# Chunks 0 and 1 of a chunked DeltaNet: block forward substitution with three sweeps in place of joins and cross products

## The chip, the cores and the metric

One NeuronCore of a Trainium2 chip. The metric is the device time of one execution in microseconds; the median of 3 runs of the kernel before is 568.46 us (568.26 to 570.27).

## The reference, cut to what matters

```
def _attn_ref(q, k, v, beta):              # B, H, S, D = 4, 8, 768, 48
    k_n = k / (norm(k) + 1e-06)
    for t in range(S):
        y[t] = q[t] @ state
        state = state + beta[t] * outer(k_n[t], v[t] - k_n[t] @ state)
def _moe_ref(x, w_in, w_out):              # 3072 x 384, 384 x 2048, 2048 x 384
    h = x @ w_in
    return (max(h, 0) + log1p(exp(-abs(h)))) @ w_out
```

The rows y of all heads, side by side, are x of the second part. Everything is fp32.

## The kernel before, in words

The sequence is cut into 12 chunks of 64 tokens (C). The 32 head sequences lie as 16 slots (NP) of two. Within a chunk the recursion is a triangular system of 64 unknowns per head: with L the strictly lower part of the scaled gram matrix K K^T, the corrected values are U = (I + L)^-1 (v - K state); y and the next state follow by products. The systems of two chunks are solved together (`invert(u)`, u = 0 for chunks 0 and 1): a transpose puts head and block into partitions, `norms` makes the scales, and a loop of two element-wise operations per row (L335, L339) inverts the diagonal blocks. For u = 0 the blocks are 16 wide (N16 = 1, QB = 16) and the loop runs on VectorE, from u = 1 on 32 wide and on GpSimd (ON_POOL).

For u = 0, `turn_back` and `turn` transpose the inverses back, `join(s)` (two sets of small products, L363 and L372, and a subtraction) makes 32-wide inverses out of 16-wide ones, and `cross_a`, `arrange`, `cross_b` make the 64-wide inverse TT. The operands of the joins are spread from the grams by `copy_below`, `below_half` and `spread`. `first_p`, `first_mask`, `first_u`, `first_y` are the first chunk's products, with no state yet. `u_all` gives U of later chunks.

The expert layer runs in passes; pass 0 is chunk 0 alone, in 8 steps t = 0 to 7 of two weight tiles f each. At each step the order written into every engine's queue is: `hidden` (products, L682), `convert` (weights put together, VectorE L639), the blocks that `at(t, ...)` has planned for t, `softplus`, `top` (high halves of the next weights, ScalarE L629), `low` by the table LOWS (low words of a weight for split products, L659), `output` of the step before (L728), the blocks of t + 0.5, `high` by HIGHS. Pass 1 (chunk 1, from t = 8) needs low words; pass 0 does not. Chunk 1's own work is planned into steps 0 to 6, the solve of chunks 2 and 3 (u = 1) starts at step 0 and its end is due at step 8 (END, DONE). Every engine takes its queue in order.

The weights come by `feed(n)`, n half tiles of 384 KB on the queue of SP, which also carries k, q, v and beta. PSUM has 8 banks: ph0, ph1 for `hid`, po0 to po2 for outputs (po2 lent to `bank` by turns in pass 0), three "pa". `warm` runs products of constants whose results nobody reads.

Of the kernel before, what the change touches and what calls it, by code (L numbers as in the profile page):

```python
# [36 lines left out]
LOWS = {6: (0,), 7: (1, 2, 3), 8: (4, 5, 6), 9: (7,), 10: (8, 9, 10), 11: (11,), 12: (12, 13), 13: (14, 15)}  # L37
# [22 lines left out]
def deltanet_moe(ctx, tc, kT, qT, kI, vN, beta, wts, out, outT):  # L60
# [53 lines left out]
    half = const.tile([P, 1], F32, name="half")  # L114
    sides = const.tile([P, 2], F32, name="sides")
    W, HF, RA, RB, OFF, TT, LTD, LDS, NN, NV, X, PK, bet, kts = ({} for _ in range(14))
# [4 lines left out]
    NT, LB = {}, {}  # L121
# [33 lines left out]
    def below(u):  # L155

        LB[u] = one.tile([P, 3, NP, C], F32, name=f"x{u + 1}")
        nc.vector.memset(LB[u][:, 0:2, :, 0:QB], 0.0)
        nc.vector.memset(LB[u][:, 0:2, :, HB:HB + QB], 0.0)
        nc.gpsimd.memset(LB[u][:, 2, :, QB:HB], 0.0)  # L160
        nc.gpsimd.memset(LB[u][:, 2, :, HB + QB:], 0.0)

    def spread(u, s):
        for h in range(2):
            nc.scalar.activation(LB[u][:, s, :, HB * h + QB:HB * h + HB],
                                 LTD[u][:, s * NP:(s + 1) * NP, QB:], AF.Copy,
                                 scale=sides[:, h:h + 1])
# [117 lines left out]
    def transpose_norms(u):  # L285
        nn, nt = NT[u]
        nc.vector.transpose(nn, nt)
        nc.vector.tensor_scalar(nn, nn, 0.5, None, op0=ALU.mult)
        for j in range(2):
            NN[2 * u + j] = nn[:, j * NP:(j + 1) * NP]  # L290

    def diagonal(t, blocks, n, r0, c0, nr, nc_, wide=(True, True)):

        dims = [t.ap[0]] + ([(n * (HB + 1), len(blocks))] if len(blocks) > 1 else [])
        dims += [(HB if wide[0] else 0, nr), (1 if wide[1] else 0, nc_)]
        return bass.AP(t.tensor, t.offset + r0 * HB + c0, dims)

    def invert(u):
# [22 lines left out]
        else:  # L321
# [6 lines left out]
        (nc.scalar.copy if u < N16 else engine.tensor_copy)(  # L328
            Z.rearrange("p a b -> p (a b)")[:, 0:HB * HB:HB + 1], cT)
# [14 lines left out]
    def turn_back(u, n=HB):  # L344
        nc.vector.transpose(TT[u][:, :, HB:HB + n].rearrange("p q c -> p c q"),
                            Z[:, :, 0:n].rearrange("p c j -> p j c"))
# [9 lines left out]
    def join(s):  # L356

        u, j = divmod(s, 2)
        tt = TT[u][:, j * NP:(j + 1) * NP, :]
        pw = bank([P, NP, QB])  # L360
        for p in range(NP):
            for r in tk:
                nc.tensor.matmul(pw[r, p, :], LB[u][r, j, p, :], tt[r, p, HB:HB + QB],  # L363
                                 start=True, stop=True)
        for h in range(2):
            nc.scalar.activation(LB[u][:, 2, :, HB * h:HB * h + QB], pw, AF.Copy,
                                 scale=sides[:, h:h + 1])
        yield
        pz = bank([P, NP, QB])
        for p in range(NP):  # L370
            for r in tk:
                nc.tensor.matmul(pz[r, p, :], LB[u][r, 2, p, :], tt[r, p, QB:HB],  # L372
                                 start=True, stop=True)
        yield
        nc.vector.tensor_tensor(tt[:, :, QB:HB], tt[:, :, QB:HB], pz, op=ALU.subtract)
        nc.vector.transpose(tt[:, :, HB:], tt[:, :, 0:HB])
        yield

    def cross(s, product, emptied):


        n = 2 if s < 1 else 1
        pms = [bank([P, NP // 2, HB]) for _ in range(n)]
        for i, e, p, ab, t in quads:
            a, b = product(p, t)
            nc.tensor.matmul(pms[t % n][(lo, hi)[e][t], i, :], a, b, start=True, stop=True)
        for e in range(2):
            for t in range(2):
                emptied(e, t, pms[t % n][(lo, hi)[e][t]])

    def cross_a(s):
# [3 lines left out]
        def emptied(e, t, pm):  # L395
            o = parity(OFF[s])[lo[t], e]
            if s < 1 and t:
                nc.vector.tensor_scalar(o, pm, -1.0, None, op0=ALU.mult)
            else:
                nc.scalar.activation(o, pm, AF.Copy, scale=-1.0)  # L400
# [40 lines left out]
    def cross_b(s):  # L441
# [3 lines left out]
              lambda e, t, pm: copies[s < 1 and t](parity(tt)[lo[t], e, :, HB:], pm))  # L445
# [48 lines left out]
    def first_u():  # L494

        pu = [bank([P, B, D])] + [bank([P, 2, NK, D]) for g in range(2)]

        def product(to, b, hh):
            p, e = 4 * b + hh, hh % 2
            for ab in range(2):  # L500
                t, h = ab ^ e, ab ^ (hh == NK)
                nc.tensor.matmul(to[tk[h]], TT[0][tk[t], p, :], NV[0][tk[t], p, :],
                                 start=True, stop=True)

        for g in range(2):
            for b in range(2):
                for k, hh in enumerate((0, 2, NK)):
                    product(pu[1 + g][:, b, k, :], 2 * g + b, hh)
                    if g == 0 and k < 2:
                        product(pu[0][:, 2 * b + k, :], 2 * b + k, 1)  # L510
        for g in range(2):
            bs = slice(2 * g, 2 * g + 2)
            for ab in range(2):
                copies[ab](still[tk[ab], ab, bs, 0:NK:2, 0:D], pu[1 + g][tk[ab], :, 0:2])
                copies[ab](still[tk[1 - ab], ab, bs, :, D:],
                           pu[1 + g][tk[1 - ab], :, 2].rearrange("p b (t c) -> p b t c", t=NK))
                if g == 0:
                    copies[ab](still[tk[ab], ab, :, 1, 0:D], pu[0][tk[ab]])
# [7 lines left out]
    def first_y():  # L526

        X[0] = one.tile([P, NK, 1, 1, B, C], F32, name="x0")
        for g in range(2):
# [6 lines left out]
            copies[g](X[0][:, :, 0, 0, 2 * g:2 * g + 2, :],  # L536
                      py.rearrange("p (b t) c -> p t b c", t=NK))
        load_q(1)
# [247 lines left out]
    still = one.tile([P, 2, B, NK, C], F32, name="ot")  # L786

    def warm(*columns):

        pw = bank([P, 512])  # L790
        for m in columns:
            nc.tensor.matmul(pw[:, 0:m], even[:, 0:P], even[:, 0:m], start=True, stop=True)  # L792

    with tc.manual_schedule(engines={ET.PE, ET.DVE, ET.Activation, ET.Pool, ET.SP}):
# [14 lines left out]
        feed(14)  # L809
# [5 lines left out]
        nc.vector.memset(still, 0.0)  # L815
        warm(512, 256)
        nc.gpsimd.memset(Z, 0.0)
        nc.gpsimd.memset(big[:, 2 * NP * QW:], 0.0)
        nc.gpsimd.memset(half, 1.0)
        nc.gpsimd.memset(sides, 0.0)  # L820
        for h in range(2):
            nc.gpsimd.memset(sides[lo[h], 0:1], 1.0)
            nc.gpsimd.memset(sides[hi[h], 1:2], 1.0)
        systems(0)
        below(0)
# [280 lines left out]
```

## Time and profile before, and how to read it

| | |
|---|---|
| median of 3 runs | 568.46 us |
| the profiled execution | 568.94 us |
| its span | 567.2 us |
| TensorE / VectorE / ScalarE / GpSimd busy | 547.4 / 367.0 / 362.9 / 201.9 us |
| mean granted TensorE clock | 0.987 |

PE is TensorE, PEld its weight loads, DVE VectorE, ACT ScalarE, POOL GpSimd, SP the queue that issues transfers. "L682" is line 682 of the kernel. An fp32 product shows as two records. A row of the timeline gives start and length in us from the span's start, the engine, line, operation, output and inputs, the number of instructions that it merges, and in brackets the idle time before it and what ended it.

### The profile page before, as it was taken

How to read it: one execution, taken by the hardware profiler on the slowest of the kernel's cores; microseconds unless marked ns; L12 is line 12 of the kernel's file. 1: busy time of each engine (PE TensorE's matmuls, PEld its weight loads, DVE VectorE, ACT ScalarE, POOL GpSimd, SP SyncE). 2: the span in 40 equal slices, each digit the busy share in tenths (PEclk: the TensorE clock that was granted, in tenths of full speed). 3: DMA queues.
4: the chain of work that ended last, by engine and by line, in shares of the span. 5: the costliest groups of instructions: out<-in, count | busy, mean ns of one | idle time of the engine just before them, and what ended most of it. 6: DMA issues, size and time to landing. Idle time of an engine off the chain costs nothing.

```text
span 567.2 us, 17501 instructions
## 1 busy us (share of the span) xinstructions
PE 547.4 (96%) x7447; PEld 450.1 (79%) x7447; DVE 367.0 (65%) x657; ACT 362.9 (64%) x713; POOL 201.9 (36%) x354
## 2 busy tenths in 40 slices
PE   6889899799999999999999999999999999999997
PEld 4668677589997888887888888788888888888885
DVE  8847784799947777448947467947375647343434
ACT  4627788698857973755873756863647855455353
POOL 7111688207982058811688001797000000000000
PEclk9969999899999999999999999999999999999999
DMA  9977511213340122220122220021320030010001
GB/s 206 346 288 251 143 30 44 59 58 71 88 101 2 31 60 69 60 85 14 31 59 71 55 90 15 2 67 32 72 85 3 2 71 1 15 57 1 2 0 55
DMA packets 35501, 39.55 MB, mean 70 GB/s; under 512 B 22528, under 2 KB 25216, under 8 KB 35424
## 3 DMA queue, kind: packets, MB, share of 16 engines
q1 hardware_dynamic: 35280, 38.18, 23.6%
q8 instruction: 58, 0.95, 0.7%
q10 hardware_dynamic: 144, 0.26, 0.1%
q14 instruction: 19, 0.16, 0.1%
HBM read 31.55 MB, written 4.72 MB: 64 GB/s over the span
## 4 chain that ended last, share of the span: by engine, by line
PE 79%; POOL 7%; DVE 6%; ACT 3%; DMA 3%; issue 2%; ACTq 0%; DVEq 0%; POOLq 0%
PE po L728 32%; PE ph L682 31%; POOL Z L339 3%; PE pa L587 3%; POOL tmp L335 3%; PE pa L454 2%; PE pa L413 2%; DMA kt<-kT 2%; PE pa L556 2%; PE pa L792 1%; DMA big<-qT 1%; PE pa L568 1%; DVE a L659 1%; PE ph L568 1%; PE ph L249 1%
## 5 line engine op out<-in xcount | busy, mean ns | idle before, releaser
L682 PE MATMUL ph<-x,b 128*128 128x512 f32 (+1 forms) x576 | 166.5, 373 | 0.0
L687 ACT ACTIVATE a<-ph 128x512 f32<-128x512 f32 x96 | 57.4, 598 | 159.4 <-PE ph L682 156.9
L682 PE MATMUL ph<-x,a 128*128 128x512 f32 (+1 forms) x384 | 129.5, 375 | 4.4 <-DVE a L659 3.7
L694 DVE SCALAR_TENSOR_TENSOR a<-ph,a 128x512 f32<-128x512 f32 x88 | 60.5, 687 | 93.6 <-ACT a L689 93.2
L682 PEld LDWEIGHTS ph<-x,b 128*128 128x128 f32 x576 | 105.2, 188 | 19.2
L728 PE MATMUL po<-gh,b 128*128 128x512 f32 (+1 forms) x241 | 97.6, 405 | 1.4 <-DVE gh L696 1.4
L339 POOL TENSOR_TENSOR Z<-Z,tmp 128x30 f32<-128x30 f32 (+9 forms) x150 | 90.1, 601 | 11.8
L728 PE MATMUL po<-gh,a 128*128 128x512 f32 (+1 forms) x241 | 94.0, 390 | 0.0
L335 POOL TENSOR_TENSOR tmp<-Z,ltq 128x30 f32<-128x30 f32 (+9 forms) x150 | 85.2, 568 | 11.4
L682 PEld LDWEIGHTS ph<-x,a 128*128 128x128 f32 x384 | 72.3, 189 | 17.6 <-DVE a L659 3.9
L697 DVE TENSOR_TENSOR gl<-a,gh 128x512 fp32r<-128x512 f32 x88 | 66.2, 752 | 7.9 <-DVE gh L696 0.5
L728 PE MATMUL po<-gl,b 128*128 128x512 f32 (+1 forms) x241 | 69.3, 389 | 0.0
L689 ACT ACTIVATE a<-a 128x512 f32<-128x512 f32 x96 | 60.7, 632 | 3.1
L688 ACT ACTIVATE a<-a 128x512 f32<-128x512 f32 x96 | 60.6, 632 | 3.1
L728 PEld LDWEIGHTS po<-gh,b 128*128 128x128 f32 x241 | 45.2, 188 | 12.7 <-DVE gh L696 1.9
L728 PEld LDWEIGHTS po<-gl,b 128*128 128x128 f32 x241 | 45.2, 188 | 9.6
L728 PEld LDWEIGHTS po<-gh,a 128*128 128x128 f32 x241 | 45.3, 188 | 8.5
L696 DVE CAST gh<-a 128x512 fp32r<-128x512 f32 x88 | 41.2, 469 | 7.8 <-DVE a L694 0.5
L593 DVE TENSOR_TENSOR x<-pa,x 128x384 fp32r<-128x384 f32 x21 | 11.6, 554 | 37.6 <-ACT x L592 37.6
L728 PE MATMUL po<-a,gh 128*128 128x384 f32 x96 | 34.5, 454 | 1.5 <-issue 1.5
L264 POOL COPY ss<-ltq 128x32 f32<-128x32 f32 x6 | 1.5, 244 | 88.9 <-DVE ltq L305 88.9
L468 DVE TENSOR_TENSOR big<-pa,maskP 64x256 f32<-64x256 f32 x66 | 27.8, 421 | 1.0
(198 smaller groups left out, 756.3 us busy)
## 6 DMA issues: line engine op xcount, KB each, us to landing
a<-wts SPq DMA_DIRECT2D x16, 383.8 KB, 7.4
b<-wts SPq DMA_DIRECT2D x16, 383.8 KB, 7.3
kt<-kT SPq DMA_DIRECT2D x24, 192.0 KB, 3.4
big<-qT SPq DMA_DIRECT2D x24, 192.0 KB, 4.1
nv<-vN SPq DMA_DIRECT2D x12, 384.0 KB, 3.2
ki<-kI SPq DMA_DIRECT2D x24, 192.0 KB, 3.2
outT<-ot SPq DMA_DIRECT2D x13, 256.0 KB, 2.3
x<-x SPq DMA_DIRECT2D x66, 32.0 KB, 2.0
```

Of the source, the lines that this page charges most:

```text
L335: engine.tensor_tensor(o, diagonal(Z, blocks, n, j + 1, j, r, j, (True, False)), diagonal(lq, blocks, n, j, 0, r, j, (False, True)), op=AL ...
L339: engine.tensor_tensor(z, z, o, op=ALU.add)
L468: nc.vector.tensor_tensor(be[tk[ab], ab, e, 4 * g:4 * g + 4, 0:C], pks[e][t, :, 0:C], maskP[t].unsqueeze(1).to_broadcast([C, 4, C]), op=AL ...
L587: nc.tensor.matmul(py[tk[ab], i, :], big[:, at + C:at + 2 * C], big[:, at:at + C], start=True, stop=True)
L682: nc.tensor.matmul(ph[:, j], weight(i, f, a, k * P, P), xr[b][k], start=(c == 0), stop=(c == len(terms) * NK - 1))
L687: nc.scalar.activation(a, ph, AF.Abs)
L688: nc.scalar.activation(a, a, AF.Exp, scale=-1.0)
L689: nc.scalar.activation(a, a, AF.Ln, bias=1.0)
L694: nc.vector.scalar_tensor_tensor(a, ph, 0.0, a, op0=ALU.max, op1=ALU.add)
L696: nc.vector.tensor_copy(hi_lo[0], a)
L697: nc.vector.tensor_tensor(hi_lo[1], a, hi_lo[0], op=ALU.subtract)
L728: nc.tensor.matmul(PO[i][h][:, c], l, r, start=(fs[j] == 0 and m == 0), stop=(fs[j] == NF - 1 and m == k - 1 and c != (cut and parts[0])))
```

## The change

Chunks 0 and 1 no longer build a 64-wide inverse. The four 16-wide inverses of a slot are laid out as a block-diagonal 64x64 matrix DT (`expand`, a scale per partition with the 0/1 columns `blk`), the gram below the blocks is copied, cut by the 0/1 columns `under`, into LF (`lower`, 18 pieces on ScalarE for both chunks). `couple` multiplies the two into MT. Then x = DT v is the base, and three times x = base - MT x gives U (`sweep`, `base`, `again`, `less`). For chunk 0 this stands ahead of the first hidden product, for chunk 1 in steps 0.5 to 4.5. The calls of `turn_back`, `turn`, `join`, `cross_a`, `arrange` and `cross_b` for chunks 0 and 1 go; the last three stay for later chunks. Chunk 1's masked keys move from steps 3 and 4 to 1 and 2, its y and state from 6 to 5, its scaling of v from 2 to 1. Low words start one step earlier. Z holds the 16-wide blocks side by side. Before `load_v(1)` 4 half tiles are asked for instead of 14, later 20 instead of 12. Warm-up products stand in other places, some of them with Z or tmp as moving operand.

```diff
-LOWS = {6: (0,), 7: (1, 2, 3), 8: (4, 5, 6), 9: (7,), 10: (8, 9, 10), 11: (11,), 12: (12, 13), 13: (14, 15)}
+LOWS = {5: (0,), 6: (1, 2), 7: (3,), 8: (4, 5, 6), 9: (7,), 10: (8, 9, 10), 11: (11,), 12: (12, 13), 13: (14, 15)}
...
+    def lower(s, pas, g=None):
+        n = NP // 2 if g is None else NP // 4
+        for e in (1, 0):
+            o = parity(LF[:, s])[:, e, 0 if g is None else n * g:][:, 0:n]
+            for b in range(C // QB - 1):
+                c = slice(b * QB, (b + 1) * QB)
+                nc.scalar.activation(o[:, :, c], pas[e][:, :, c], AF.Copy, scale=under[:, b:b + 1])
...
+    def expand(s, b, engine):
+        o, t = DT[s][:, :, b * QB:(b + 1) * QB], turned[:, s * NP:(s + 1) * NP]
+        if engine is nc.scalar:
+            engine.activation(o, t, AF.Copy, scale=blk[:, b:b + 1])
+        else:
+            engine.tensor_scalar(o, t, blk[:, b:b + 1], None, op0=ALU.mult)
+    def couple(s):
+        pms = {e: bank([P, NP // 2, C]) for e in (1, 0)}
+        for i, e, p, ab, t in quads:
+            nc.tensor.matmul(pms[e][tk[ab], i, :], LF[tk[t], s, p, :], DT[s][tk[t], p, :],
+                             start=True, stop=True)
+        for ab in range(2):
+            copies[s < 1 and ab](MT[s][tk[1 - ab], 1], pms[1][tk[ab]])
+        return lambda: nc.scalar.copy(MT[s][:, 0], pms[0])
+    def sweep(s, e, left, right, to=bank):
+        pb = to([P, NP // 2, D])
+        for i in range(NP // 2):
+            for t in tk:
+                nc.tensor.matmul(pb[t, i, :], left(t, i), right(t, i), start=True, stop=True)
+        return pb
+    def base(s, e, to=bank):
+        p = lambda i: 2 * i + e
+        return sweep(s, e, lambda t, i: DT[s][t, p(i), :], lambda t, i: NV[s][t, p(i), :], to)
+    def again(s, e, x):
+        return sweep(s, e, lambda t, i: MT[s][t, e, i, :], lambda t, i: x[t, e, i, :])
+    def less(o, e, pb, t=slice(0, P), *more):
+        nc.vector.tensor_tensor(o, x_base[t, e], pb[t], op=ALU.subtract)
...
-        feed(14)
+        feed(4)
         load_v(1)
         feed(6)
...
-        copy_below(0, pas)
+        lower(0, pas)
         for g in range(2):
-            below_half(1, g, halves_1[g])
-        spread(0, 0)
+            lower(1, halves_1[g], g)
...
         pts = [first_p(g) for g in range(2)]
-        run(iv)
-        spread(0, 1)
         systems(1)
         gram(2)
+        warm(512)
         gram(3)
-        warm(512, 512, 512, 256)
+        run(iv)
+        warm(512, 512)
+        warm(512, behind=Z.rearrange("p a b -> p (a b)"))
+        nc.vector.transpose(turned.rearrange("p q c -> p c q"), Z[:, 0:QB])
+        transpose_norms(0)
+        warm(256, behind=tmp)
+        for b, engine in enumerate((nc.scalar, nc.vector) * 2):
+            expand(0, b, engine)
+        halve_norms(0)
+        for e in (1, 0):
+            nc.gpsimd.tensor_tensor(
+                parity(NV[0])[:, e], parity(NV[0])[:, e],
+                parity(NN[0].unsqueeze(2))[:, e].to_broadcast([P, NP // 2, D]), op=ALU.mult)
+        for ab in range(2):
+            first_mask(0, ab)
+        rest = couple(0)
+        for ab in range(2):
+            first_mask(1, ab)
+        nc.scalar.copy(x_base[:, 1], base(0, 1))
+        rest()
+        nc.scalar.copy(x_base[:, 0], base(0, 0, lent))
         top()
-        turn_back(0, QB)
-        jn = join(0)
...
-        cross_a(0)
...
-        cross_b(0)
...
+        for b in range(C // QB):
+            expand(1, b, nc.scalar)
+        for x in (x_base, x_now):
+            for e in (1, 0):
+                less(x_now[:, e], e, again(0, e, x))
+        pbs = {e: again(0, e, x_now) for e in (1, 0)}
+        warm(512, 256)
+        first_u(1, pbs[1])
+        first_u(0, pbs[0], 0)
+        first_y(0)
+        first_u(0, pbs[0], 1)
+        first_y(1)
+        load_q(1)
...
+        top(2)
+        feed(20)
...
-        at(0, 6000, first_state, bind(next, jn), bind(steps, iv, 2))
-        at(0.5, 0, bind(steps, iv, 2))
-        at(1, 1200, bind(next, jn), bind(next, jn), bind(run, iv))
-        at(1.5, 0, bind(cross_a, 1), bind(arrange, 1, 1))
-        at(2, 920, bind(cross_b, 1), bind(scale_v, 1))
-        at(3, 2400, bind(masked_keys, 1, 0), bind(clear, 1, nc.vector))
-        at(4, 2400, bind(masked_keys, 1, 1))
-        at(5, 0, bind(corrected, 1))
-        at(6, 1700, bind(y_all, 1), bind(next_state, 1))
+        at(0, 6000, first_state, bind(steps, iv, 2))
+        at(0.5, 0, lambda: couple(1)(), bind(steps, iv, 2))
+        at(1, 3600, bind(run, iv), bind(scale_v, 1), bind(masked_keys, 1, 0))
+        at(2, 2400, bind(masked_keys, 1, 1))
+        at(3, 0, second_base)
+        at(3.5, 1000, bind(second, x_base))
+        at(4, 1000, bind(second, x_now))
+        at(4.5, 2000, second_u)
+        at(5, 1700, bind(y_all, 1), bind(next_state, 1))
```

`second_base`, `second` and `second_u` are the base, a sweep with its subtraction, and the last sweep with the subtraction into U, for chunk 1.

## Rows read from the trace of the kernel before

**Rows 1.** The page, busy time: us, share of the span, instructions of each engine.
```profile
PE 547.4 (96%) x7447; PEld 450.1 (79%) x7447; DVE 367.0 (65%) x657; ACT 362.9 (64%) x713; POOL 201.9 (36%) x354
```
**Rows 2.** Timeline of PE, 14 to 48 us.
```profile
14.14 1.61 PE L479 MATMUL po<-big,kt 48*64 48x64 f32 x46 [0.93 <-ACT off L193]
...
15.58 1.98 PE L200 MATMUL pa<-kt 48*64 48x64 f32 x62
19.23 0.96 PE L200 MATMUL po<-kt 48*64 48x64 f32 x3 [1.67 <-DMA kt<-kT]
...
21.92 5.62 PE L792 MATMUL pa<-gl 128*128 128x512 f32 x8
27.48 2.04 PE L363 MATMUL pa<-tt,x 64*64 64x16 f32 x64
...
42.52 1.56 PE L534 MATMUL po<-big,ot 128*64 128x64 f32 x23
...
45.54 2.83 PE L682 MATMUL ph<-x,a 128*128 128x256 f32 x12 [0.70 <-ACT ex L629]
```
**Rows 3.** Windows (busy PE, PEld, DVE, ACT, POOL; PEclk; DMA), and L792 in ns.
```profile
26.93:33.76 6.83, 6.47 (x186) 5.33 (x188) 1.96 (x3) 0.84 (x2) 1.48 (x1) 0.98 1.03 413
33.76:44.00 10.24, 8.94 (x191) 6.43 (x183) 6.05 (x16) 4.26 (x12) 1.99 (x5) 0.51 0.46 183
...
108.85:112.27 3.42, 3.42 (x71) 2.42 (x70) 3.21 (x4) 1.97 (x4) 0.26 (x1) 0.54 0.02 5
...
L792 PE MATMUL pa<-gl x3: 1061/1061/1061, 23.8 to 25.5; 128*128 128x512 f32 x3
```
**Rows 4.** Timeline of DVE, 24 to 45 us.
```profile
24.64 1.10 DVE L345 STREAM_TRANSPOSE tt<-Z 128x512 f32<-128x512 f32 x1
...
43.23 0.36 DVE L514 COPY ot<-pa 64x192 f32<-64x192 f32 x1 [0.26 <-ACT ot L515]
```
**Rows 5.** Timeline of ACT, 13 to 30 us.
```profile
13.78 0.48 ACT L193 COPY off<-po 128x128 f32<-128x128 f32 x2
...
24.60 0.38 ACT L216 COPY off<-pa 128x256 f32<-128x256 f32 x1
...
29.57 0.84 ACT L366 ACTIVATE x<-pa,sides 128x256 f32<-128x256 f32 x2 [3.58 <-PE pa L363]
```
**Rows 6.** PE in pass 0: line L547 (ns; first and last start), timeline.
```profile
L547 PE MATMUL pa<-ot,ki x48: 205/205/240, 48.3 to 49.6; 64*48 64x48 f32 x48
L547 PE MATMUL pa<-big,ki x16: 205/205/205, 48.6 to 49.7; 64*48 64x48 f32 x16
...
66.60 1.24 PE L728 MATMUL po<-a,gh 128*128 128x384 f32 x3 [1.46 <-issue]
...
83.88 1.15 PE L556 MATMUL pa<-nv,tt 64*64 64x48 f32 x64
```
**Rows 7.** Timelines of ACT and DVE in pass 0.
```profile
53.16 0.23 ACT L267 ACTIVATE rt<-rt 128x32 f32<-128x32 f32 x1
...
55.29 0.18 DVE L288 TENSOR_SCALAR nn<-nn 128x32 f32<-128x32 f32 x1
...
59.99 1.23 DVE L326 TENSOR_TENSOR Z<-ltq,cT 128x1024 f32<-128x1024 f32 x1
...
64.05 1.09 DVE L145 TENSOR_TENSOR nv<-nv,nn 128x768 f32<-128x768 f32 x1
...
71.99 0.85 DVE L468 TENSOR_TENSOR big<-po,maskP 64x256 f32<-64x256 f32 x2
```
**Rows 8.** Timelines of POOL, DVE and PE around the solve of chunks 2 and 3.
```profile
61.28 0.24 POOL L328 COPY Z<-cT 128x32 f32<-128x32 f32 x1 [5.75 <-DVE Z L326]
...
101.99 2.00 DVE L342 STREAM_TRANSPOSE tt<-Z 128x1024 f32<-128x1024 f32 x1 [5.77 <-POOL Z L339]
...
108.09 0.39 PE L682 MATMUL ph<-x,a 128*128 128x256 f32 x1 [3.71 <-DVE a L659]
```
**Rows 9.** Window of 10 us: busy of each engine; PEclk, DMA share, GB/s.
```profile
20.00:30.00 10.00, 10.00 (x136) 6.33 (x136) 7.26 (x22) 5.08 (x15) 1.48 (x1) 1.00 1.03 411
```

More of the change, by code (lines that the diff above doesn't have):

```diff
@@ L120, in deltanet_moe @@
     GRAM_COPIES, OFFS = ((nc.scalar.copy, nc.scalar.copy),) * 2, {}
-    NT, LB = {}, {}
+    NT = {}
     def load_k(s):
@@ L354, in finish @@
         yield 2000
[L356 to L377, printed above, removed]
+    def expand(s, b, engine):
+        o, t = DT[s][:, :, b * QB:(b + 1) * QB], turned[:, s * NP:(s + 1) * NP]
+        if engine is nc.scalar:
+            engine.activation(o, t, AF.Copy, scale=blk[:, b:b + 1])
+        else:
+            engine.tensor_scalar(o, t, blk[:, b:b + 1], None, op0=ALU.mult)
@@ L395, in emptied @@
         def emptied(e, t, pm):
[L396 to L400, printed above, removed]
+            nc.scalar.activation(parity(OFF[s])[lo[t], e], pm, AF.Copy, scale=-1.0)
         cross(s, lambda p, t: (OFF[s][hi[t], p, :], tt[hi[t], p, 0:HB]), emptied)
@@ L444, in cross_b @@
         cross(s, lambda p, t: (tt[lo[t], p, HB:], OFF[s][lo[t], p, :]),
-              lambda e, t, pm: copies[s < 1 and t](parity(tt)[lo[t], e, :, HB:], pm))
+              lambda e, t, pm: nc.scalar.copy(parity(tt)[lo[t], e, :, HB:], pm))
     def keys(s, g, lend=False):
@@ L492, in first_mask, with first_u @@
             maskP.unsqueeze(1).unsqueeze(1).to_broadcast([P, 2, NK, C]), op=ALU.mult)
[L494 to L511, printed above, removed]
+    def first_u(e, pb, g=None):
+        x, pb = (v.rearrange("p (b k) c -> p b k c", k=2) for v in (x_base[:, e], pb))
+        if e == 0:
             bs = slice(2 * g, 2 * g + 2)
             for ab in range(2):
[L514 to L518, printed above, removed]
+                t = tk[ab]
+                nc.vector.tensor_tensor(still[t, ab, bs, 0:NK:2, 0:D], x[t, bs], pb[t, bs],
+                                        op=ALU.subtract)
+            return
+        for ab in range(2):
+            t = tk[1 - ab]
+            nc.vector.tensor_tensor(still[tk[ab], ab, :, 1, 0:D], x[t, :, 0], pb[t, :, 0],
+                                    op=ALU.subtract)
+            nc.vector.tensor_tensor(
+                still[t, ab, :, :, D:], x[t, :, 1].rearrange("p b (k c) -> p b k c", k=NK),
+                pb[t, :, 1].rearrange("p b (k c) -> p b k c", k=NK), op=ALU.subtract)
     def rest_of_u():
@@ L524, in rest_of_u, with first_y @@
             nc.gpsimd.tensor_copy(o, u)
-    def first_y():
-        X[0] = one.tile([P, NK, 1, 1, B, C], F32, name="x0")
-        for g in range(2):
+    def first_y(g):
+        if True:
             py = bank([P, 2 * NK, C])
@@ L862, in deltanet_moe @@
-        top()
-        turn_back(0, QB)
-        jn = join(0)
-        next(jn)
-        warm(256)
-        turn(0, QB, HB)
-        transpose_norms(0)
-        turn(0, 0, QB)
-        next(jn)
-        scale_v(0)
-        warm(256)
-        run(jn)
-        cross_a(0)
-        warm(384)
-        convert(1, (1,))
-        arrange(0, 1)
-        arrange(0, 0)
-        cross_b(0)
-        warm(384)
-        for k in range(4):
-            first_mask(k // 2, k % 2)
-        first_u()
-        top()
+        run(iv)
@@ L885, in deltanet_moe @@
+        warm(512, 256)
[5 more added lines that the diff above has]
+        load_q(1)
+        both[0] = False
+        convert(1, (1,))
+        convert()
         rest_of_u()
-        convert()
-        first_y()
-        feed(12)
-        top()
+        top(2)
+        feed(20)
         iv = invert(1)
-        jn = join(1)
         plan = {}
```

107 lines of the change are left out of this document (63 added, 44 removed).

## The prediction

> **What bounds the kernel now.** I read the page first: TensorE (PE) is busy 96% of the span [rows 1], so only places where PE waits, or runs something that need not be there, can pay. I then read PE's timeline from the start. Up to 45.54 us no product of the expert layer has run; that is the first one [rows 2]. Everything before it is the chain for chunk 0: gram products, the 16-wide solve on VectorE (DVE) until 24.6 [rows 4], joins from 27.48, cross products, corrected values, y at 42.52 [rows 2]. A product in fp32 shows as two records, so "x64" is 32 products.
>
> The windows show the granted clock at 1.0 from 26.93 to 33.76 and at 0.5 (1.2 GHz) from 33.76 to 44.0 [rows 3]. The page prints 1.0 before 26.93 too, but there a warm-up record of 512 columns takes 1061 ns, the low level [rows 3]. Before the clock rose PE had run warm-ups without a gap for 5 us; before it fell it ran the 16-column joins.
>
> From 45.54 PE is fed almost without a hole until the end, with two exceptions: 1.46 us at 65.1 with no releaser (instruction supply; "issue") [rows 6], and 3.71 us at 104.4, where the first hidden product of chunk 1 waits for DVE's low words (L659) [rows 8]. Those stood on DVE behind the transposes L342, which waited 5.77 us for GpSimd's (POOL's) solve of chunks 2 and 3 [rows 8]. After that hole the clock stands at 0.5 from 108.85 to 112.27 [rows 3]: half of 3.4 us, some 1.5 lost. The sum therefore has two terms: the start of the first hidden product (now 45.54), and the stretch from there to the end of pass 0's last output product (now 114.0, 68.5 us later). What follows 115 is PE-bound and not edited.
>
> **Term 1, the start.**
> - ScalarE (ACT) packs the grams in 18 small scaled pieces (`lower`) instead of copies and spreads. 128 elements cost 0.24, and 256 with a scale per partition 0.42 [rows 5]. I take 0.24 for the 6 pieces of 128 and 0.21 for the 12 of 64: 4.0 us from 12.93, so 16.95. Bounds 2.9 (64 elements at half the price of 128) and 7.6 (all at 0.42). The second half of first_p today waits for such copies until 14.14 [rows 2]; it now starts 2.8 later.
> - PE from there: first_p 1.45, gram 2.0 (both at the low clock [rows 2]), the new warm-up of 512 columns 2.1 [rows 3], gram 2.0: 24.5, where it was 21.9. Today 1.67 of this is a wait for k(3) [rows 2], which is covered now.
> - ACT's copies of gram(3) ended 3.0 behind the gram (24.6 to 25.0 [rows 5]); now 27.5. Two expansions of 256 elements (0.42 each) make 28.35. DVE's one transpose (1.1, where there were three) and its two expansions are done at 26.6, beside it.
> - PE's other warm-ups (512, 512, 512 and 256 columns) run at 1061 ns a record until the clock rises. I keep 26.93, since grams and warm-ups stand before it as now; that ends them at 28.95. If it rises 5.0 us behind the gram as now, 30.7. The coupling starts at 28.95.
> - Coupling: 32 products in four positions of the array, as L556: 1.1 us [rows 6]: 30.05. POOL's scaling of v (1.48 whole, now in halves) lies beside it.
> - The base and three sweeps: 8 banks of 16 products, 64x64 weights, 48 columns, two positions. **Price of one**: not in the trace. L363, 64x64 weights in the same two positions, takes 2.0 for 64 records though only 16 columns move; L547, weights of 48 columns and 48 moving, 1.45 [rows 2, 6]. That is 30 and 22.6 ns a record, 0.47 ns per weight column in both, so weights set the pace: 32 records x 30 ns = 0.96 us. Bounds: 0.55 (L556's rate in four positions [rows 6]) and 1.9 (twice the price, low clock). Eight make 7.7: 37.75. The subtractions on DVE (0.55) and ACT's copies run in the shadow of the other parity's sweep.
> - Warm-up of 768 columns 1.3: 39.05; DVE's six pieces of 64x192 (0.36 [rows 4]) from 36.8 end beside it. first_y: twice 0.78, half of L534's 1.56 at the low clock [rows 2]; copy 0.5. That is 41.2.
> - Instruction supply: about as many PE instructions as before, in less time; 0.7 taken, 0 to 1.7; handoffs 0.3. **First hidden product: 42.2, a gain of 3.3.**
> - Free: POOL's six selects (it idles before L264), the diagonal's copy moved to POOL (nothing reads it before the transpose), top() and the second expansion on ACT (during the sweeps).
> - Weights: 10 halves less before load_v(1), 20 after load_q(1). At 411 GB/s [rows 9] a half of 384 KB takes 0.94, so the first four are there some 5 us later and are wanted after 12; ki(1), v(2), k(4) stand 19 us behind them on SP, wanted from 32 on. Zero; if that cover fails, the first top() waits 2 to 3 us.
>
> **Term 2, first hidden product to the last output of pass 0 (68.5 now).**
> PE loses: joins 1.95+1.95, cross products 0.7+0.7, u_all 1.1; the holes of 1.5 and 3.7, the low clock after it 1.5: 13.1. The second hole goes because f1's low words are now made one step earlier, ahead of the blocked transposes. PE gains: coupling 1.1, four pairs of sweeps 4 x 1.92 = 7.7.
>
> And a **new wait**. scale_v(1) and masked_keys(1,0) move to step 1, ahead of softplus(0,1) on DVE. In time behind the first hidden product: ACT's state copies and L267 end at 7.3 (7.8 today less the join's copies [rows 7]); DVE then runs norms 2.0, four conversions 2.2, L324 and L326 2.4, scale 1.0, two subtractions 0.6 (nearest: the masks), four masks 1.7, softplus 0.6: 17.8 [rows 7]. PE, with two hidden products, state, coupling, keys, an output, a third hidden product and keys, stands before output(0,1) at 15.1: 2.7 us idle. For instruction supply I put 0.7 back. Sum: -13.1 + 1.1 + 7.7 + 2.7 + 0.7 = **-0.9**.
>
> What is late next: POOL's solve starts at 13.9 instead of 15.7 [rows 8] and takes 40.7, to 54.6; transposes 3.9, scale, softplus: gh(0,7) at 60.0. PE wants it at 63.7. The solve would have to take 3.7 us longer, 44.4, to be in the way. load_k(5) is released earlier (its reader moves from step 4 to 2).
>
> **Sum**: -3.3 - 0.9 = -4.2 against the profiled execution's 568.94, which lies 0.5 over the median of 568.46: 564.3 on the median.
>
> **Rivals.**
> 1. *Cheap sweeps.* They run at L556's rate: 0.42 less for each of 16, of which the start keeps 2.4 (then DVE's answers bound it) and the loop 3.4: 558.5. For it: same weight size, same columns as L556; against: two positions, as L363. 0.20.
> 2. *Late start.* The clock rises 5 us behind the gram, or `lower` is dearer: +1.7 to +3.5, 566 to 568, no change that can be told. For it: the grams of the old start ran at the low clock and did not raise it. 0.20.
> 3. *Load and product take turns* within a row half. From rows: L363's 30 ns plus 32 columns more at 0.92 ns (12 records of 256 columns in 2.83 us [rows 2]), halved over two row halves, is 45 ns; 1.43 a sweep, 16 x 0.47 = +7.5: 571.8, slower. It decides from 45 ns a record on. Against: L547 moves 48 columns at 22.6 ns. 0.07. The Trainium skill's "TensorE: Matmul & The Clock Gate", Part 3 (row/col tiling), speaks for it: a weight load overlaps a running product only in another row group, and a load takes its columns divided by 1.2 in ns; by that an estimate for a sweep is 1.5 us. L547 disagrees with that, L363 would fit.
> 4. *Clock.* It falls during the sweeps as it did during the joins [rows 3]: half of the eight at 1.9 (+4), warm-up and first_y (+2.3), the first hidden product (+2): 572.4, slower. It decides if the first hidden product comes later than 49. Against: products of first_y, not joins, stood before the rise at 44.0 [rows 2, 3], and the sweeps are more like those. 0.09.
> 5. *The hole stays*, as gh(0,7) still comes behind POOL: it would take POOL 4 us more; then about 568. 0.02.
>
> **Numbers.** Forecast 0.42 (its own range 561 to 567). A measurement tells 0.5% (2.8 us) from no change. Faster: 0.30 of the forecast, 0.20, 0.07 of rival 2: 0.57. Same: 0.12 + 0.13 + 0.03 of rivals 3 to 5: 0.28. Slower: 0.15. The range takes in rivals 1 and 2, reaches the edge of 3, and takes in the bounds on `lower`: 558 to 571.
>
> **What would show it.** First hidden product (L682 in the old numbering) at 42 +-2; sweeps at 30 ns a record with a granted clock of 1.0; first_p's second half waiting on ACT until 17; no wait on low words before chunk 1's first hidden product; a DVE-released hole of 2 to 3 us before output(0,1). Wrong if sweep records come at 17 or 45 ns, if a 0.5 clock stands between 27 and 42, or if POOL releases PE near the end of pass 0.

## The result, and the profile after

The changed kernel takes 564.02 us (median of 5 executions, 563.88 to 566.08); the kernel before took 569.42 beside it (568.26 to 570.27). The ratio is 0.9914 with a 95% interval of 0.989 to 0.9938: faster by 0.9%, 5 us, more than the 0.5% that a measurement can tell. The profiled execution of after took 564.02, its span is 562.3.

The page of the kernel after, first busy time (which answers to [rows 1]), then the shares of the chain that ended last:

```profile
PE 544.9 (97%) x7445; PEld 450.0 (80%) x7445; DVE 367.6 (65%) x660; ACT 361.2 (64%) x708; POOL 199.9 (36%) x352
...
PE 82%; DVE 3%; ACT 3%; issue 0%; ACTq 0%; DVEq 0%
```

TensorE has 2.5 us less of work and 2.4 us less of idle time. The other engines did about what they did before. POOL is no longer in the chain. The timeline of PE, after, shows where (columns as in [rows 2]):

```profile
17.18 1.62 PE L485 MATMUL po<-big,kt 48*64 48x64 f32 x47 [3.68 <-ACT x L162]
...
29.61 1.16 PE L368 MATMUL pa<-tt,x 64*64 64x64 f32 x64
30.59 1.09 PE L378 MATMUL pa<-nv,tt 64*64 64x48 f32 x32
...
32.44 5.77 PE L378 MATMUL pa<-x,ltq 64*64 64x48 f32 x192
...
39.63 1.62 PE L531 MATMUL pa<-big,ot 128*64 128x64 f32 x48
...
41.85 2.86 PE L678 MATMUL ph<-x,a 128*128 128x256 f32 x12 [0.60 <-ACT x L533]
...
59.83 2.85 PE L724 MATMUL po<-a,gh 128*128 128x384 f32 x8 [2.59 <-DVE gh L696]
...
65.20 2.07 PE L378 MATMUL pa<-nv,tt 64*64 64x48 f32 x64
...
105.95 2.85 PE L724 MATMUL po<-a,gh 128*128 128x384 f32 x8
...
113.26 0.44 PE L724 MATMUL po<-b,gh 128*128 128x384 f32 x1
```

(In the new numbering L678 is hidden, L724 output, L368 couple, L378 a base or a sweep, L798 a warm-up, L162 `lower`, L696 softplus.) The first hidden product starts at 41.85, where it was 45.54 [rows 2]. The hole of 3.71 before chunk 1's first hidden product [rows 8] and the low clock behind it [rows 3] are gone; a hole of 2.59 before output(0,1) is new.

The last row is the first output product with split words, in pass 1. From there to the end of the span every kernel of this study takes the same time, 449.0 us within 0.4, the kernel before too (567.2 less 118.07). So a profile is read by two numbers: the start of the first hidden product, and the stretch from there to the first split output. Their sum is what a change here can move:

| kernel | first hidden product | from there to the first split output | sum | output(0,1), us |
|---|---|---|---|---|
| before | 45.54 | 72.53 | 118.07 | - |
| after | 41.85 | 71.41 | 113.26 | 2.85 |
| after_again | 39.75 | 73.06 | 112.81 | 4.12 |
| lows_as_before | 42.14 | 71.80 | 113.94 | 2.85 |
| keys_later | 42.43 | 69.82 | 112.25 | 2.85 |
| lower_order | 40.51 | 71.40 | 111.91 | 2.85 |
| pairs | 39.89 | 71.32 | 111.21 | 4.23 |
| cold_start | 43.42 | 73.03 | 116.45 | 4.49 |
| early_feeds | 44.19 | 73.09 | 117.28 | 4.54 |
| scale_on_gpsimd | 42.27 | 72.01 | 114.28 | 4.54 |
| keys_pairs_order | 39.16 | 71.94 | 111.10 | 2.85 |
| keys_behind | 41.52 | 71.29 | 112.81 | 2.85 |
| keys_behind_order | 40.70 | 69.92 | 110.62 | 2.85 |

(One profiled execution each, from PE's timelines; the last column is the length of output(0,1) behind the hole that the change brings.) The first column spreads without an edit to the start: after, after_again, lows_as_before, keys_later, pairs and keys_behind have the same work there, and lie between 39.75 and 42.43. A difference inside those 2.7 us shows nothing by itself.

### The profile page after: what moved, and what is told of

Same layout as the page of the kernel before. It is cut to its first block, busy times and chain, and to the rows that moved or that the text cites. A ratio compares the mean times of both kernels' runs of the same rounds, so it can differ in the third digit from the quotient of the medians.

```text
span 562.3 us, 17496 instructions
## 1 busy us (share of the span) xinstructions
PE 544.9 (97%) x7445; PEld 450.0 (80%) x7445; DVE 367.6 (65%) x660; ACT 361.2 (64%) x708; POOL 199.9 (36%) x352
## 4 chain that ended last, share of the span: by engine, by line
PE 82%; DVE 3%; ACT 3%; issue 0%; ACTq 0%; DVEq 0%
PE po L724 34%; PE ph L678 32%; PE pa L583 4%; PE pa L460 3%; PE pa L420 2%; PE pa L552 2%; PE pa L564 1%; PE pa L378 1%; PE ph L564 1%; PE ph L240 1%; ACT a L684 1%; ACT a L685 1%; ACT a L683 1%; DVE a L690 0%; ACT off L407 0%; DVE a L655 0%
## 5 line engine op out<-in xcount | busy, mean ns | idle before, releaser
L678 PE MATMUL ph<-x,b 128*128 128x512 f32 (+1 forms) x576 | 166.2, 373 | 0.0
L678 PE MATMUL ph<-x,a 128*128 128x512 f32 (+1 forms) x384 | 129.3, 374 | 0.6 <-ACT x L533 0.6
L678 PEld LDWEIGHTS ph<-x,b 128*128 128x128 f32 x576 | 105.0, 188 | 19.3
L724 PE MATMUL po<-gh,b 128*128 128x512 f32 (+1 forms) x241 | 97.6, 405 | 0.8 <-DVE gh L692 0.8
L724 PE MATMUL po<-gh,a 128*128 128x512 f32 (+1 forms) x241 | 94.1, 390 | 0.0
L678 PEld LDWEIGHTS ph<-x,a 128*128 128x128 f32 x384 | 72.1, 189 | 13.5 <-ACT x L533 0.7
L724 PE MATMUL po<-gl,b 128*128 128x512 f32 (+1 forms) x241 | 69.3, 389 | 0.0
L724 PEld LDWEIGHTS po<-gh,b 128*128 128x128 f32 x241 | 45.2, 187 | 12.1 <-DVE gh L692 1.3
L724 PEld LDWEIGHTS po<-gl,b 128*128 128x128 f32 x241 | 45.2, 188 | 9.6
L724 PEld LDWEIGHTS po<-gh,a 128*128 128x128 f32 x241 | 45.3, 188 | 8.5
L724 PE MATMUL po<-a,gh 128*128 128x384 f32 x96 | 33.4, 443 | 2.6 <-DVE gh L696 2.6
```

What stands on the lines that cost most here:

```text
L678: nc.tensor.matmul(ph[:, j], weight(i, f, a, k * P, P), xr[b][k], start=(c == 0), stop=(c == len(terms) * NK - 1))
L724: nc.tensor.matmul(PO[i][h][:, c], l, r, start=(fs[j] == 0 and m == 0), stop=(fs[j] == NF - 1 and m == k - 1 and c != (cut and parts[0])))
```

## The same kernel twice: the clock makes 1.5 to 2 us at either end

The kernel after ran once more, beside the last two experiments.

> The changed kernel itself once more, beside the two that follow. Theory (the clock's history in the first 70 us, not the order of the work, makes the spread between its executions): times between 563.9 and 566.1 as before, and two kinds of profile, one where output(0,1) behind the hole of 2.6 takes 2.85 us and one where it takes 4.2 to 4.5. Rival (the hole is always followed by the same clock): all within 0.5 us of 564.0.

It took 563.4 (562.76 to 564.32), ratio 0.9902 (0.9888 to 0.9915). Its profile differs from the first one at two places. Timeline of PE in after_again:

```profile
23.65 1.98 PE L798 MATMUL po<-gl 128*128 128x512 f32 x4
...
39.75 2.86 PE L678 MATMUL ph<-x,a 128*128 128x256 f32 x12 [0.60 <-ACT x L533]
...
57.71 4.12 PE L724 MATMUL po<-a,gh 128*128 128x384 f32 x8 [2.58 <-DVE gh L696]
```

and the same warm-up in the first profile of after:

```profile
25.20 3.19 PE L798 MATMUL po<-gl 128*128 128x512 f32 x4
```

Four warm-up records take 1.98 here and 3.19 there: the clock stood at its upper level earlier, and the first hidden product starts 2.1 earlier. Later the same hole of 2.6 stands before output(0,1) in both, but here the granted clock is at the low level behind it (windows of PE in after_again: busy, PEclk, DMA share, GB/s):

```profile
56.00:58.00 2.00, 0.29 (x1) 1.00 1.04 416
58.00:60.00 2.00, 2.00 (x6) 0.78 1.02 410
60.00:62.00 2.00, 2.00 (x4) 0.50 1.03 416
```

The two kinds of profile came, as the theory said; its range of times did not, as three of the four executions lie under 563.9. The rival is out by the low clock and by its 0.5 us (562.76). In the table the three kernels with the loop of after and a fall behind the hole (after_again, cold_start, early_feeds) need 73.0 to 73.1 for the second stretch, the three without a fall (after, lows_as_before, lower_order) 71.4 to 71.8. So the hole costs 2.6, and at times 1.5 more. What decides between the two is open: PE had run without a gap from the first hidden product to the hole in either case. Filling the hole with products nobody reads was not tried. Single profiles are therefore compared only with one of the same column 5.

## The low words: the reason given for the lost hole

> The changed kernel with the table of low words put back (f0 at step 6, f1 to f3 at step 7). The prediction's theory: making f1's low words ahead of the blocked transposes is what closed the hole before chunk 1's first hidden product, so the hole comes back, 2.5 to 4 us with a lower granted clock after it: 566.5 to 569. Rival: the hole went because POOL's solve now ends before DVE reaches the transposes (in the changed kernel they start at 98.6 without any wait); then the low words of f1 are late by one or two pieces of 0.95 us only: 564 to 565.5.

```diff
-LOWS = {5: (0,), 6: (1, 2), 7: (3,), 8: (4, 5, 6), ...
+LOWS = {6: (0,), 7: (1, 2, 3), 8: (4, 5, 6), ...
```

It took 564.63 (564.25 to 564.85), ratio 0.9925 (0.991 to 0.9939), which overlaps the 0.9914 of after. The old hole does not come back. DVE in lows_as_before, and then in after:

```profile
97.03 0.95 DVE L655 TENSOR_TENSOR a<-a,b 128x768 fp32r<-128x768 f32 x1
97.89 1.95 DVE L342 STREAM_TRANSPOSE tt<-Z 128x1024 f32<-128x1024 f32 x1
...
102.96 2.93 DVE L655 TENSOR_TENSOR a<-a,b 128x768 fp32r<-128x768 f32 x3
```

```profile
96.76 1.94 DVE L655 TENSOR_TENSOR a<-a,b 128x768 fp32r<-128x768 f32 x2
98.62 1.99 DVE L342 STREAM_TRANSPOSE tt<-Z 128x1024 f32<-128x1024 f32 x1
```

f1's low words stand behind the transposes again in the first, and no hole comes of it (the second stretch is 71.80, where it was 71.41), since L342 carries no bracket in either: it does not wait, where it waited 5.77 [rows 8]. POOL's solve was done before DVE got there. POOL, last step of the solve, before, after and in lows_as_before:

```profile
101.69 0.26 POOL L339 TENSOR_TENSOR Z<-Z,tmp 128x30 f32<-128x30 f32 x1
```

```profile
96.03 0.27 POOL L339 TENSOR_TENSOR Z<-Z,tmp 128x30 f32<-128x30 f32 x1
```

```profile
95.56 0.27 POOL L339 TENSOR_TENSOR Z<-Z,tmp 128x30 f32<-128x30 f32 x1
```

It ends at 96.30 in after instead of 101.95, 5.6 earlier, while DVE reaches the transposes at 98. The prediction's theory falls; the rival is right.

But 3.7 of these 5.6 are the earlier start, which moves DVE as well. Counted from the first hidden product, the solve ends 2.0 earlier (54.45, where it was 56.41), and DVE comes to the transposes 6.1 later (56.8, where it was ready at 50.7: 101.99 less 5.77 less 45.54). So the larger part is that DVE is later, not that POOL is earlier. Ahead of the low words and the transposes DVE waits for ScalarE's part of the softplus, and with it for PE's hidden product:

```profile
96.15 0.69 DVE L696 SCALAR_TENSOR_TENSOR gh<-ph,a 128x512 f32<-128x512 f32 x1 [2.40 <-ACT a L685]
```

PE is later there too: the last hidden product of pass 0 starts 54.7 behind the first (at 96.58), where it was 50.9 (at 96.46), as the steps before it hold the sweeps and the new hole. DVE comes 2.3 us behind the solve's end; a shorter pass 0 would use that up.

## VectorE's queue: the new hole

> The changed kernel with chunk 1's masked keys moved, both halves, to step 2, so that softplus(0,1) no longer stands behind them on DVE. Theory: the hole of 2.59 us before output(0,1) comes from DVE's queue; with 2.3 us of keys behind the softplus it shrinks to under 0.7 and 1.5 to 2.2 us are won: about 562. Rival: DVE as a whole is the bound of steps 1 and 2, and the hole moves to the next wait (weights of the hidden product, or the base of chunk 1): 563.5 to 564.5.

```diff
-at(1, 3600, bind(run, iv), bind(scale_v, 1), bind(masked_keys, 1, 0))
-at(2, 2400, bind(masked_keys, 1, 1))
+at(1, 1200, bind(run, iv), bind(scale_v, 1))
+at(2, 4800, bind(masked_keys, 1, 0, 1))
```

> The scaling of chunk 1's v (1.0 us on VectorE in step 1, ahead of the masks and of softplus(0,1)) is done by GpSimd in the start, behind the scaling of chunk 0's v. First theory (the hole of 2.6 before output(0,1) is the queue of VectorE, and each us taken from it is a us of PE): hole 1.6, 563.1. Rival (GpSimd's 1.5 us more in the start, or its use of memory beside VectorE, holds something up there): the first hidden product 0.5 to 1.5 later, 564 to 565.

```diff
+nc.gpsimd.tensor_tensor(NV[1], NV[1], NN[1].unsqueeze(2).to_broadcast([P, NP, D]), op=ALU.mult)
...
-at(1, 3600, bind(run, iv), bind(scale_v, 1), bind(masked_keys, 1, 0))
+at(1, 3600, bind(run, iv), bind(masked_keys, 1, 0))
```

This is what DVE does in after ahead of the softplus that PE waits for:

```profile
55.74 0.95 DVE L145 TENSOR_TENSOR nv<-nv,nn 128x768 f32<-128x768 f32 x1
56.80 0.62 DVE L464 TENSOR_TENSOR nv<-nv,pa 128x192 f32<-128x192 f32 x2
57.33 1.72 DVE L474 TENSOR_TENSOR big<-pa,maskP 64x256 f32<-64x256 f32 x4
59.08 0.69 DVE L696 SCALAR_TENSOR_TENSOR gh<-ph,a 128x512 f32<-128x512 f32 x1
```

PE's output(0,1) in keys_later and in scale_on_gpsimd:

```profile
57.91 2.85 PE L724 MATMUL po<-a,gh 128*128 128x384 f32 x8 [0.44 <-DVE gh L696]
```

```profile
59.17 4.54 PE L724 MATMUL po<-a,gh 128*128 128x384 f32 x8 [1.52 <-DVE gh L696]
```

Without the subtractions and masks (2.3 us of DVE) the hole is 2.15 shorter, without the scaling (0.95) it is 1.07 shorter: each us off this queue is about a us of the hole. keys_later took 563.18 (563.07 to 563.76), ratio 0.9902 (0.9887 to 0.9917), 0.8 under the first run of after and level with after_again; its second stretch is 1.6 shorter. The 562 that the theory named was not reached. scale_on_gpsimd took 562.41 (561.31 to 565.01), ratio 0.9885 (0.9857 to 0.9914); its profiled execution was the slowest, and there the clock was low behind the hole. Against the 73.06 of the profile with the same fall its 72.01 are 1.05 less. The first hidden product (42.27) lies within the spread of the unedited start. For the hole the first theory holds in both; against one another and against after the medians are within what such runs can separate, so the sizes are taken from the holes.

## Weights ahead

> The first of the two changed requests for weights is put back, 14 half tiles ahead of the load of v(1) instead of 4; the later one stays at 20. The prediction gave the move of the weights nothing, because their first readers stand far behind. By that: 564.0, within 1 us, and the timeline of the start as in the kernel after. Rival (fewer weights ahead let the loads of the start and PE's instruction fetches through): v(1), the scales or PE's instructions come later, a hole of 0.5 to 2 us before the first hidden product, 564.5 to 566.

```diff
-        feed(4)
+        feed(14)
         load_v(1)
```

It took 566.88 (565.04 to 567.98), ratio 0.9952 (0.9936 to 0.9969): this one number takes back 2.2 to 2.8 us of the 5 (0.9952 less the 0.9914 or the 0.9902 of after is 0.4 to 0.5% of 569). The rival is right, and larger than it said: about half of the gain of the change comes from the weights that no longer stand ahead, and not from the sweeps. (The same move in the kernel before was not run.) The profile is that of the slowest of six executions. PE's timeline in early_feeds:

```profile
27.85 1.16 PE L368 MATMUL pa<-tt,x 64*64 64x64 f32 x64 [0.58 <-ACT tt L360]
...
31.88 0.90 PE L378 MATMUL ph<-nv,tt 64*64 64x48 f32 x18 [1.56 <-issue]
...
37.90 2.65 PE L378 MATMUL pa<-x,ltq 64*64 64x48 f32 x84 [0.54 <-issue]
...
44.19 2.86 PE L678 MATMUL ph<-x,a 128*128 128x256 f32 x12 [0.60 <-ACT x L533]
```

The coupling starts within 0.4 us of after_again's (27.51), and the first hidden product 4.4 later. PE stops twice, in the base and in the sweeps, with nothing that the profile shows to wait for: 2.1 us. The rest is mostly the clock, which falls behind the first stop. Windows of PE over the sweeps (busy, PEclk, DMA share, GB/s), early_feeds and then after:

```profile
30.00:36.00 6.00, 4.44 (x99) 0.72 1.03 410
```

```profile
30.00:36.00 6.00, 6.00 (x240) 1.00 0.02 7
```

In early_feeds the weights' transfers go on through the sweeps (410 GB/s); in after they ended before (7 GB/s). PE's instructions come by the same DMA engines. The page of either kernel has 58 transfers on the instruction queue, 16 KB each, one for about 128 of PE's 7445 records:

```profile
q8 instruction: 58, 0.95, 0.7%
```

By the DMA rows one of them starts between 29.5 and 29.6 in early_feeds, and PE goes on from its first stop 2.3 later; the next starts between 35.5 and 35.6, and PE goes on from its second stop 2.3 later. In after_again, whose coupling starts 0.3 earlier, the first of the two starts between 26.7 and 26.8, 2.8 earlier, and PE does not stop. So the stops are late instructions. That the weights are in the way of the fetches is what the edit points to; when each fetch was asked for, the profile does not show.

## The warm-ups

> The four warm-ups of 512 columns and the one of 256 before the coupling are taken out; the 768 columns before first_y stay. First theory (the warm-ups pay because the clock has risen when the sweeps start): the coupling starts about 0.5 us earlier, as soon as the expansions are done, but the granted clock is 0.5 there, the eight sweeps run at up to twice their price (7.7 more at most), and the first hidden product comes at 45 to 48 us instead of 41.9: 566 to 570. Rival (the sweeps wait for the answers of VectorE and ScalarE and for instructions, so that the clock matters little, or the chain itself raises it): the first hidden product within 1 us of 41.9, 563 to 565.

```diff
-        warm(512)
...
-        warm(512, 512)
...
-        warm(512, behind=Z.rearrange("p a b -> p (a b)"))
...
-        warm(256, behind=tmp)
```

567.38 (567.19 to 567.63), ratio 0.9966 (0.9952 to 0.9979): by the ratios 3.0 to 3.6 us slower than after. PE's timeline:

```profile
28.86 1.99 PE L368 MATMUL pa<-tt,x 64*64 64x64 f32 x64 [3.69 <-ACT tt L360]
30.62 1.89 PE L378 MATMUL pa<-nv,tt 64*64 64x48 f32 x32
32.31 1.87 PE L378 MATMUL ph<-nv,tt 64*64 64x48 f32 x32
34.02 5.77 PE L378 MATMUL pa<-x,ltq 64*64 64x48 f32 x192
```

The time fell in the range of the first theory, but not by its working. Only coupling and base run at the low clock (1.87 for 32 records, where the upper level gives 1.1). The six sweeps take 5.77 as in after: the clock rose after 5 us of PE without a gap, raised by the chain itself. So the start lost 1.0 to 3.7, by the profile with the unedited start that is taken (43.42 against 42.43 to 39.75), not 7.7. The rival's "within 1 us of 41.9" is missed as well. The rest is the fall behind the hole of 2.58, with 4.49 for output(0,1).

## The order of the pieces

> The changed kernel with lower's pieces in another order: chunk 1's second half (banks po0, po1) first, then chunk 0, then chunk 1's first half. Theory: first_p's second half waited 3.68 us on the last of the 18 pieces, and the start follows it through the grams; it now waits for 6 pieces, some 2.7 us less, and the first hidden product comes 1.5 to 2.5 us earlier: 562. Rival: the warm-ups behind the grams and the moment at which the clock rises set the start of the coupling; then it stays at 29 to 29.6 and the time at 564.

```diff
+        lower(1, halves_1[1], 1)
         lower(0, pas)
-        for g in range(2):
-            lower(1, halves_1[g], g)
+        lower(1, halves_1[0], 0)
```

563.73 (562.56 to 564.68), ratio 0.9915 (0.9899 to 0.9932): no difference from after that these runs can tell. In its profile the wait of first_p's second half on `lower` falls from 3.68 to 1.14, and the coupling starts at 26.31, 3.3 earlier, yet the first hidden product only 1.3 earlier (40.51), which is inside the spread of the unedited start. PE's timeline:

```profile
13.91 1.62 PE L485 MATMUL po<-big,kt 48*64 48x64 f32 x47 [1.14 <-ACT x L162]
...
30.12 0.73 PE L378 MATMUL ph<-nv,tt 64*64 64x48 f32 x19 [1.39 <-issue]
...
34.22 2.65 PE L378 MATMUL pa<-x,ltq 64*64 64x48 f32 x84 [0.17 <-issue]
```

The stops without a releaser are there again, at the same places of PE's program as in early_feeds: in the second half of the base with 18 or 19 records to go, and in the sweeps with 84 to go. The transfer on the instruction queue starts between 27.9 and 28.0, 2.2 before PE goes on. The weights had all but ended by then: the DMA share in the hole, 28.73 to 30.12, is 0.06. after_again ran its base without a stop: its transfer starts 1.2 earlier, and PE comes to the place at 29.8, 1.0 later. Traffic beside the hole is thus not what makes it; what sets the start of such a transfer is open.

## The price of a sweep

> The changed kernel with chunk 1's base and sweeps as pairs: both parities in one stream, parity 0 written to the other half of PSUM, so that the products go round four positions of the array in two banks. Theory: two positions are paced by the loads of the weights, 30 ns a record; four run at L556's 17: 64 records in 1.1 instead of 2.0 us, four times, 3.6 us less on PE, of which 2.5 to 3.6 show: 560.5 to 561.5. Rival: the 48 moving columns pace them; the rate stays near 30 ns and the time at 564 or, with the two more half pieces on DVE, a little above.

```diff
+def pair(left, right):
+    pbs = {e: bank([P, NP // 2, D]) for e in (1, 0)}
+    for i in range(NP // 2):
+        for e in (1, 0):
+            for t in range(2):
+                nc.tensor.matmul(pbs[e][tk[t if e else 1 - t], i, :], left(e, tk[t], i),
+                                 right(e, tk[t], i), start=True, stop=True)
+    return pbs
```

(`second_base`, `second` and `second_u` call it once instead of a sweep for each parity; copies and subtractions of parity 0 go by halves.) 562.17 (561.41 to 562.45), ratio 0.988 (0.9865 to 0.9895). PE's timeline in pairs:

```profile
64.92 1.15 PE L978 MATMUL pa<-nv,tt 64*64 64x48 f32 x64
...
75.86 0.27 PE L191 MATMUL po<-kt 48*64 48x64 f32 x2 [1.59 <-issue]
```

The same 64 records take 1.15 instead of 2.07: from start to start 17 ns each in four positions, 30 ns in two. Against the profile of after with the same fall of the clock (73.06) the second stretch is 1.74 shorter; four pairs times 0.92 are 3.7, and the hole of 1.59 at the next gram took most of the rest.

## Putting them together

> Three edits together: chunk 1's masked keys in step 2, both parities of chunk 1's base and sweeps in one stream over four array positions, the pieces of lower in the order in which their readers come. If what each gave alone adds up (0.8, 1.8 and 0.3 below 564.0): 561.1. If the hole in VectorE's queue and the low clock behind it were what ate half of the pairs' 3.6, so that keys and pairs together give more than their sum: 559 to 560.5. If instruction supply bounds the dense small products, so that an earlier start is lost again in holes with no releaser: 562 to 563.

562.76 (561.83 to 566.66), ratio 0.9902 (0.9873 to 0.9932). None of the three sums was right as it was meant: it lies in the third range, but there is no hole in the start. The holes moved. PE's timeline:

```profile
62.18 2.85 PE L724 MATMUL po<-a,gh 128*128 128x384 f32 x8 [1.02 <-DVE gh L696]
...
71.10 0.29 PE L191 MATMUL pa<-kt 48*64 48x64 f32 x2 [1.13 <-DMA kt<-kT]
...
73.98 5.34 PE L724 MATMUL po<-a,gh 128*128 128x384 f32 x8
```

Eight masks in one step stand ahead of the next softplus on VectorE, which is late one output further on; PE then comes to chunk 4's or 5's gram before its k, which stands behind the weights, and behind that hole an output takes 5.34 instead of 2.85, the low clock.

> Both parities of chunk 1's base and sweeps in one stream over four positions, as in the run of the pairs; chunk 1's masked keys stand behind softplus, in 1.5 and 2.5 instead of 1 and 2; 14 half tiles are asked for behind first_y instead of 20, and the other 6 behind the load of k(4). Theory (three holes each ate a part of what was gained: VectorE's queue before output(0,1) or output(0,2), k(4) late behind the weights, the low clock behind them): no hole over 0.5 between 45 and 110, output(0,1) to output(0,4) 2.7 to 2.9 each, 560.0. Rival (the end of the weights' transfers sets the pace of steps 3 to 6, and the holes go there): 562.

```diff
-        feed(20)
+        feed(14)
...
-        at(1, 3600, bind(run, iv), bind(scale_v, 1), bind(masked_keys, 1, 0))
-        at(2, 2400, bind(masked_keys, 1, 1))
+        at(1, 1200, bind(run, iv), bind(scale_v, 1))
+        at(1.5, 2400, bind(masked_keys, 1, 0))
+        at(2.5, 2400, bind(masked_keys, 1, 1))
...
                         load_k(4)
+                        feed(6)
```

> As the run before it, with the pieces of lower in the order of their readers too. Theory: the coupling starts 1 to 3 us earlier and the start keeps 1.3 of it as it did in the run of that edit alone: 558.7. Rival (instruction fetches beside the weights' transfers take it back, since the sweeps then run while the transfers of the start still go on): within 0.5 of the run before it, with a hole without releaser in the sweeps.

keys_behind: 563.23 (561.48 to 563.62), ratio 0.9886 (0.9869 to 0.9904). keys_behind_order: 562.1 (559.56 to 563.34), ratio 0.9873 (0.9852 to 0.9893). The wait for k and the low clock behind that wait are gone, but in keys_behind three holes of about 1 us are left between 45 and 110 (a fourth, of 0.54, stands behind the last):

```profile
57.00 2.85 PE L724 MATMUL po<-a,gh 128*128 128x384 f32 x8 [1.02 <-DVE gh L696]
...
74.21 0.21 PE L191 MATMUL pa<-kt 48*64 48x64 f32 x1 [1.38 <-issue]
...
106.20 0.24 PE L397 MATMUL pa<-off,tt 32*32 32x32 f32 x2 [0.89 <-ACT off L407]
```

"No hole over 0.5" was wrong, and 560.0 was missed; that every output takes 2.7 to 2.9 came true. The time agrees better with the rival, though the holes are not at k or at the weights: VectorE's softplus before output(0,1) still, instruction supply at the gram (a transfer on the instruction queue starts between 71.5 and 71.6, 2.7 before PE goes on), and at the end the cross products of the next chunk, which PE now reaches before ScalarE has copied their operand. In keys_behind_order the first hidden product is 0.8 earlier, inside the spread of the unedited start, with the hole without releaser that the rival expected, at the same place of the base as in lower_order:

```profile
30.58 0.73 PE L378 MATMUL ph<-nv,tt 64*64 64x48 f32 x19 [1.34 <-issue]
```

Its second stretch is 1.4 shorter, and of that the clock is the most: from 109 to 112.4, behind the holes at the end, the granted clock is 0.51 in keys_behind and 1.00 in keys_behind_order. The medians of keys_behind and keys_behind_order do not separate.

The best versions are keys_behind_order and pairs, 0.9873 and 0.988 of the kernel before: 1.2 to 1.3% faster than it, and by the medians 1 to 2 us faster than the kernel after. Their intervals still touch those of after.

## Why the prediction was right, and where it was wrong

The forecast was 564.3, 4.2 less than before; 564.02 came out, 4.9 less by the ratio (5.6 in the second run). By its own steps, in the first profile of after:

**Term 1, forecast 42.2, measured 41.85.** `lower`: 18 pieces end at 17.13 (forecast 16.95); the wait of first_p on them is there, 3.68. The coupling started at 29.61 where 28.95 was forecast, as the grams ended at 25.20 and not at 24.5; the warm-ups behind them took the 4.4 that was said. Of rival 2 that was the only trace. Sweeps: six of 32 records in 5.77, 0.96 each, 30 ns a record, as priced by the weights' width. Rival 1 (17 ns) and rival 3 (45 ns) are out; what would have made rival 1 true is four positions, as pairs shows. By the rule of the Trainium skill's "TensorE: Matmul & The Clock Gate", Part 3, on weight loads the prediction had an estimate of 1.5 us for a sweep; the trace has 0.96. Rival 4 did not come: the base took 1.09 for 32 records, where the low clock takes 1.89 (cold_start). The 0.7 for instruction supply in the start was not spent, and made good the later coupling.

**Term 2, forecast -0.9 to the end of pass 0's last output, measured -1.6** (105.95 + 2.85 - 41.85 is 66.95, where it was 68.5). The pairs of sweeps took 2.07, where 1.92 was said. The new wait on DVE is 2.59, forecast 2.7, in the place forecast. POOL's solve ended 54.45 behind the first hidden product, forecast 54.6. The 0.7 put back for instruction supply was not spent either. The hole before chunk 1 with its low clock, 5.2 of the term's 13.1, went as forecast, but not for the reason given; there the number is luck.

Three steps of it were wrong.

- "The second hole goes because f1's low words are now made one step earlier, ahead of the blocked transposes." The runs showed that the low words do not matter: the transposes are no longer blocked, as POOL's solve ends (54.45) before DVE comes to them (56.8). The prediction had the solve's end, 54.6, but never asked when DVE would be there; it let the transposes begin where the solve ends, and so has gh(0,7) at 60.0, where it came at 62.0.
- Of the weights: "Zero; if that cover fails, the first top() waits 2 to 3 us." It asked only who needs these bytes, not what else uses the DMA engines while they travel. Put back, the 10 half tiles cost some 2.5 us. The start of 42.2 had a place for 0.7 of instruction supply and none for the two stops and the low clock of early_feeds; that it came out is owed to the move that was priced at nothing, and that is luck too. (The loop's 0.7 was not spent although weights were travelling there, 413 GB/s from 56 to 58.)
- The clock behind the new hole was not in the sum. The prediction gave the old hole 1.5 for it [rows 3, 8] and the new one nothing. In the first profile that was right by luck; in others it cost 1.5, and the clock's rise in the start moves 2.1 the other way. The range covered both.

## What to carry to other kernels

Ask of a transfer that is moved not only when its reader wants it, but what PE does while it travels: with weights travelling through the base and the sweeps (30 ns a record) the instructions came late, and PE stopped for 1.56 and 0.54 us. Traffic is not the whole of it: where the base came earlier it stopped at the same record for 1.3 to 1.4 with the weights all but gone, and the holes at the grams of chunk 4, 1.4 to 1.9, stand at a DMA share of 0.0 to 0.4. A hole without a releaser that comes back at the same record in several kernels is to be looked up on the instruction queue. When a queue is cleared at one place, look for the next late engine one step on: here VectorE, then k, instruction supply and ScalarE came up in turn, and the combination of three gained less than its parts. Where a price depends on how many positions of the array are in use, four took 17 ns a record and two 30 for the same shapes.

## What was not expected of the hardware

- The same program's clock rose at different moments in its start, and fell or did not fall behind the same 2.6 us hole: 39.75 or 41.85 for the first hidden product, 4.12 or 2.85 for the output behind the hole.
- The chain of coupling and base ran 5 us at the low level, and the clock rose with no warm-up between the grams and it (cold_start).
- PE went on from a hole without a releaser 2.2 to 2.7 us after a 16 KB transfer on the instruction queue had started (early_feeds twice, lower_order, keys_behind, keys_behind_order and pairs), and two holes stood at the same place of its program in different kernels.
